# A planned attention and gated-MLP kernel: staging buffers, load shape and planner constants

## The chip, the cores and the metric

The kernel runs on one core of a Trainium2 chip. The metric is the device time of one launch in microseconds, as the median of several runs. One execution was also recorded by the hardware profiler; all durations below come from it.

## The reference, cut to what matters

Windowed attention with sink positions, and then a gated layer on its result. q, k and v are float32; the three weight matrices are 64-bit floats.

```python
# q, k, v: (4, 8, 768, 64); n_sink = 4, window = 128
scores = q @ k.T / sqrt(64)
keep   = (column < n_sink) | (0 <= row - column < window)
a      = softmax(where(keep, scores, -1e9))
x      = (a @ v)                       # reshaped to (3072, 512)
gate   = 1 / (1 + exp(-(x @ w_gate)))  # w_gate, w_val: (512, 1536)
out    = (gate * (x @ w_val)) @ w_out  # w_out: (1536, 512)
```

## The kernel before, in words

**Units of work.** A *head* here is one attention head over 256 rows of a batch: 4 batches x 3 row blocks x 8 heads = 96 of them (`attend`, numbered `u`). The first 20 (`PLAIN`) work in plain float32, which TensorE passes over four times; the others split each operand into a high part and a low part in the fast format (`copy` makes the high part, `rest` the low part) and add the products. The gated layer runs in 8 *chunks* of rows (`CHUNKS`, `feed`), each in 12 *slices* of 128 hidden columns. Chunk 0 (`feed_whole`) uses the unsplit weights `ws`; chunks 1 to 3 (`feed_plain`) use high and low parts; chunks 4 to 7 (`feed_pair`) take two row blocks together and save one product in eight.

**Weights.** Each slice has three blocks of raw 64-bit weights (gate, value, out; 512 KB each). `decode` loads a block into a staging buffer `wst` (three of them, `B_wst`), ScalarE scales its upper words (`ws<-wst`) and shifts 16-bit pieces (`wst<-wst`; VectorE or GpSimd may do that instead), and VectorE puts the bits together in `ws`. Later `halves` and `thirds` split the blocks; the low parts go out to a DRAM scratch `wlo_d` and are fetched back into eight buffers `lo` (`fetch`) for every slice of chunks 1 to 7.

**Order.** Nothing in the code says directly what stands behind what. Each operation is given to `Plan.op` with a priority, the engines that can do it with a duration for each, and the tiles it reads and writes. `Plan.run` then plays through all engines with these durations, takes on each free engine the ready operation of best priority, and writes the resulting order down; the chip executes each engine's list in that order. Constants fix how long a result needs to reach the next engine (`LAT`, the same for all), how a transfer's landing is reckoned (`BULK`, `ISSUE`), how long an input must have been there before TensorE takes its operation ahead of others (`SURE`, `SURE_D` behind a transfer), and when an engine of second choice may take an operation (`BACKA`, `BACKV`, `HOLD`, `GAP`). Up to `WARM` (130 us) the planner puts a *fill* into TensorE's list, a product of the identity with itself (`m<-ident`, two passes), wherever TensorE would stand idle while its activity is under `FLOOR`. Stores of `wlo_d`, loads of q and k (`qkT`), of v (`vraw`, `vhl`) and of weights all go through the one queue of SyncE (SP).

**End.** A flag tells whether the general path behind the last branch is needed; it is not here. `hint` places a branch hint for TensorE, VectorE and SyncE. In the last slice (`last_slice`) the four results `xf` are stored one by one.

Names as the trace shows them: `P` probabilities, `rs` their row sums, `wt` transposed probabilities, `th` and `cv` the gated layer's intermediate values, `gh` and `gl` their high and low part, `m`, `a`, `o` PSUM tiles, `xf` attention results and, at the end, the output rows.

Of the kernel before, what the change touches and what calls it, by code (L numbers as in the profile page):

```python
# [45 lines left out]
SINKP = -2.0  # L46
SCALP = -0.5
SKSWAP = 0
WHOLE = 1
DN1 = 36  # L50
DS1 = 8.0
DR1 = 0.2
DS2 = 18.0
DR2 = 0.3
KS1 = 16.0
KR = 0.9
KS2 = 25.0
XP = -900.0
ALT = 1
LAT = 180.0  # L60
BULK = 620.0
ISSUE = 550.0
SURE = 600.0
SURE_D = 1200.0
FREE = 150.0
NEXT = dict(PE=0.0, V=60.0, A=60.0, G=60.0, Q=0.0)
# [21 lines left out]
B_lo = 8  # L88
B_w2 = 2
B_wst = 3  # L90
# [222 lines left out]
class Plan:  # L313
# [39 lines left out]
    def run(self, warm, fill_ns, fill):  # L353
# [37 lines left out]
        while events:  # L391
            now = events[0][0]
            while events and events[0][0] <= now:
# [14 lines left out]
                for x in o.after:  # L408
                    x.before -= 1
                    same = len(x.ways) == 1 and x.ways[0][0] == on  # L410
                    x.ready = max(x.ready, now + (NEXT[on] if same else LAT))
                    if on != "PE":
                        x.sure = max(x.sure, now + LAT + (SURE_D if o.dma else SURE))
                    if not x.before:
                        n += 1
                        heapq.heappush(events, (x.ready, n, ("ready", x, None)))
            for e in free:
                if free[e] > now:
                    continue
                held = []  # L420
                unsure = [] if e == "PE" else None
                while waiting[e] or unsure:
# [18 lines left out]
                    if unsure is not None and (  # L441
                        o.sure > now
                        or any(slots[k][v - 1][1] + LAT + SURE > now for k, v in need.items())
                    ):
                        unsure.append((key, o))
                        continue
# [48 lines left out]
                    if through:  # L495
                        ns += max(0.0, port - now - LEAD)
                        port = now + ns + (70.0 if e == "V" else 0.0)
# [14 lines left out]
                    if o.dma:  # L512
                        slow = BULK if o.dma > 1000.0 else 0.0
                        dma_free = max(dma_free + o.dma, end + 650 + slow + o.dma)
                        end = dma_free + 750
# [8 lines left out]
                    for x in o.after:  # L524
                        x.todo -= 1
                        x.due = max(x.due, end + LAT)
# [23 lines left out]
def kernel(  # L550
# [13 lines left out]
    w_gate, w_val, w_out = (  # L564
        w.bitcast(I32).rearrange("r (c w) -> r c w", w=2) for w in (w_gate, w_val, w_out)
    )
    B, H, S, D = v.shape
    DM, DF, _ = w_gate.shape
    DO = w_out.shape[1]
    NC = DM // 128  # L570
    NF = DF // 128
# [267 lines left out]
    WLO, LOADS, GROUPS, DECODED, READY, READY2 = (Fixed(None) for _ in range(6))  # L839

    def sinks(b, u):
        if not b:
# [7 lines left out]
            for t, x in enumerate(VS0):  # L850
                for y in range(2):
                    o = 64 * y + NS * t
                    dma(
                        u + 0.5, 91.0, lambda x=x, y=y, o=o: Q.dma_start(
# [8 lines left out]
        for o in range(0, 128, NS):  # L863
            dma(
                u, 91.0, lambda o=o: Q.dma_start(
                    out=raw()[o : o + NS], in_=v[b, :, 0:NS, :].rearrange("h p d -> p h d"),
                ), [READY2], [(raw, o)] + [VSHL[b, i] for i in range(2) if b and (b, i) in VSHL],
# [10 lines left out]
    def load(u, b, h, t0, T, prev, L, vraw, vin, qkT, plain):  # L878
# [4 lines left out]
            u, 0.75 * n * R / D, lambda: Q.dma_start(out=qkT()[0:R, 0:n], in_=qk[b, h, 0:R, c0 : c0 + n]),  # L883
# [3 lines left out]
            u, 100.0 * L, lambda: Q.dma_start(  # L887
# [4 lines left out]
    def attend(u, b, h, t0, T, XR):  # L892
# [44 lines left out]
        for t in range(T):  # L937
# [28 lines left out]
            def exp(t=t):  # L966
# [5 lines left out]
            plan.op(u, [("PE", 10 + (4 * n / 2.4 + 6 if plain else 2 * mac(n)), scores)], qk_reads, [sc, (P, t)], busy=0.5 if plain else 0.9)  # L972
            plan.op(
                u, [("V", 260 if first else 535, top)],
                [sc, (MASKS, 3), (MASKS, min(t0 + t, 2))], [sc, (P, t), (NEGM, (u, t))],
            )
            plan.op(u, [("A", 410, exp)], [], [(P, t), (rs, t)])
# [19 lines left out]
        def mul():  # L997
            for t in range(T):
# [4 lines left out]
                ("A", 200, lambda: A.activation(  # L1003
                    out=rs()[:, 0:T], in_=rs()[:, 0:T], func=AF.Copy, scale=1.0, bias=1.0e-9
                )),
                ("G", Port(213), guard(G)), ("V", Port(100), guard(V)),
# [3 lines left out]
            u, [("V", 110, lambda: V.reciprocal(out=rs()[:, 0:T], in_=rs()[:, 0:T]))], [], [rs]  # L1010
        )
        plan.op(u, [("G", Port(660), share), ("A", 720, mul), ("V", Port(555), scale)], [rs], [P])

        if not plain:
# [11 lines left out]
                u, [("V", 180, lambda: V.transpose(  # L1026
# [10 lines left out]
                u, [("G", Port(610), spread(G)), ("V", two(W), spread(V))], [turned, OWN], [sk]  # L1037
# [35 lines left out]
        plan.op(u, [("PE", 30 + (T + plain) * 110, turn)], [P], [tp, wt], busy=0.45)  # L1073
# [11 lines left out]
        plan.op(u, [("G", Port(180 + 0.9 * Z * (T - f) * 128), split)], [], [wt])  # L1085
        plan.op(u, [("G", Port(180 + 0.9 * Z * T * 128), rest_of)], [], [wt])
# [105 lines left out]
        if y:  # L1192
# [8 lines left out]
            elif not pair_of[tn]:  # L1201
# [9 lines left out]
                copy(u, W, hi, xv, read, [(H1, i), (L1, i)], plain)  # L1211
# [44 lines left out]
    def decode(prio, src, whole):  # L1256
# [6 lines left out]
        plan.op(prio, [("Q", ISSUE, lambda: Q.dma_start(out=st(), in_=src))], [], [st], dma=1456.0)  # L1263
# [16 lines left out]
                ("G", Port(1340.0), lambda: G.tensor_scalar(  # L1280
# [26 lines left out]
    def weights(f, prio):  # L1307
# [11 lines left out]
    def spare(pr, f, k, x):  # L1319
        dma(  # L1320
            pr, 728.0, lambda: Q.dma_start(
# [5 lines left out]
    def halve(pr, f, k, shape, whole, r=(), start=0.0):  # L1327
        hi, lo = slot(F32R, shape), slot(F32R, shape)
        copy(pr, 512, hi, whole, [whole, *r], [hi, (lo, 0)], start=start)
# [43 lines left out]
    def out_tiles(ci, g, T, O):  # L1373

        for j, acc in enumerate(O):
# [15 lines left out]
            dma(ci, 728.0, lambda ot=ot, r=r: Q.dma_start(out=out[r : r + 128], in_=ot()), [ot])  # L1391
# [70 lines left out]
    def fetch(pr, f, *parts):  # L1462
        got = []
        for k in parts:
            x = tile([128, 512], F32R, "lo", BUFS["lo"], p3)
            LAST[0] = dma(
                pr, 728.0, lambda x=x, k=k: Q.dma_start(
# [93 lines left out]
    def feed_pair(ci, tcs, f, O):  # L1561
# [76 lines left out]
        gh, gl = gated(pr, 512, th)  # L1638
        downs(pe, f, O, gh, gl, woh, wol, (1.3, 1.5, 1.65, 1.7))

    def last_slice(pr, pe, O, th, cv, woh, wol):
# [23 lines left out]
        hint([(gh, 1)], [(th, 1)], [wol])  # L1665
# [153 lines left out]
```

## Time and profile before

| | |
|---|---|
| median of 3 runs | 775.3 us (772.66 to 777.56) |
| the profiled execution, its own time | 774.19 us |
| its span, first to last instruction | 772.5 us |
| TensorE busy with matmuls | 749.1 us, 97% |
| VectorE, ScalarE, GpSimd busy | 607.5, 472.0, 506.1 us |
| granted TensorE clock | 0.998 |
| moved by DMA | 185.57 MB, mean 240 GB/s |

TensorE is "busy" whenever a matmul is in its pipe, so its share says that it is seldom empty. An engine's idle time counts only where TensorE, or the last store, waits for it.

### The profile page before, as it was taken

What the parts mean: (1) busy time and instruction counts of PE and PEld (TensorE: products, weight loads), DVE (VectorE), ACT (ScalarE), POOL (GpSimd) and SP (SyncE); (2) the same over time, 40 slices, a digit from 0 to 9 for tenths busy, and PEclk for the clock granted to TensorE, in tenths of its full rate; (3) what the DMA queues carried; (4) which work ended last, traced back from release to release, by engine and by line L of the source; (5) the groups of instructions that cost most, each with busy time, mean ns of one, the idle gap of its engine ahead of it and who ended that gap; (6) DMA issues with size and microseconds to landing.
All of it is one profiled execution on the core that took longest, in us unless ns stands there. A gap on an engine that the chain in (4) does not pass through costs nothing.

```text
span 772.5 us, 16296 instructions
## 1 busy us (share of the span) xinstructions
PE 749.1 (97%) x4986; PEld 674.9 (87%) x4986; DVE 607.5 (79%) x1782; ACT 472.0 (61%) x1338; POOL 506.1 (66%) x647
## 2 busy tenths in 40 slices
PE   7999999999999999999999999999999999999995
PEld 6866777998989999989999988999999999999995
DVE  5979988996999999969988889778999884433333
ACT  7879888765765777737666665457776652322221
POOL 3654676887999999937777977557976855321210
PEclk9999999999999999999999999999999999999999
DMA  6898987999999877677767777867697655677662
GB/s 165 222 297 250 323 263 234 376 307 311 342 294 319 284 220 207 200 252 231 233 224 225 242 233 222 246 196 251 193 306 249 196 159 178 217 240 211 198 205 86
DMA packets 120879, 185.57 MB, mean 240 GB/s; under 512 B 23248, under 2 KB 45264, under 8 KB 120784
## 3 DMA queue, kind: packets, MB, share of 16 engines
q1 hardware_dynamic: 120784, 184.45, 75.9%
q8 instruction: 42, 0.69, 0.4%
q14 instruction: 53, 0.43, 0.2%
HBM read 159.24 MB, written 25.17 MB: 239 GB/s over the span
## 4 chain that ended last, share of the span: by engine, by line
PE 61%; DVE 11%; DMA 6%; POOL 3%; ACT 2%; issue 2%; SPq 0%; ACTq 0%; POOLq 0%; DVEq 0%
PE m L620 34%; PE a L620 16%; PE o L620 11%; DVE ws L620 2%; DMA wst<-in_moe_w_gate_dram 1%; DMA out_dram<-w 1%; DVE P L620 1%; DVE th L620 1%; DMA vraw<-in_vt_dram 1%; DMA lo<-wlo_d 1%; DVE vhl L620 1%; POOL wt L620 1%; DVE hi L620 1%; DVE gl L620 1%; DVE xf L620 1%
## 5 line engine op out<-in xcount | busy, mean ns | idle before, releaser
L620 PE MATMUL m<-ws,ws 128*128 128x256 f32 x1536 | 290.0, 284 | 0.6 <-DVE th L620 0.2
L620 PE MATMUL m<-ws,lo 128*128 128x256 f32 x1344 | 288.6, 283 | 1.9 <-DMA lo<-wlo_d 1.3
L620 PEld LDWEIGHTS m<-ws,ws 128*128 128x128 f32 x1536 | 244.9, 189 | 13.1 <-DVE th L620 1.0
L620 PEld LDWEIGHTS m<-ws,lo 128*128 128x128 f32 x1344 | 215.0, 189 | 3.1 <-DMA lo<-wlo_d 2.3
L620 POOL TENSOR_SCALAR_AFFINE_SELECT wt<-wt 128x512 fp32r<-128x512 f32 (+3 forms) x192 | 125.9, 657 | 43.5 <-DVE wt L620 18.7
L620 POOL TENSOR_TENSOR gl<-th,gh 128x512 fp32r<-128x512 f32 (+1 forms) x34 | 38.2, 1122 | 99.6 <-ACT gh L620 82.7
L620 ACT ACTIVATE P<-P,negm_all 128x144 f32<-128x144 f32 x192 | 78.9, 412 | 28.7 <-DVE negm_all L620 26.8
L620 ACT ACTIVATE th<-m 128x256 f32<-128x256 f32 x96 | 36.6, 382 | 75.5 <-DVE th L620 71.9
L620 DVE TENSOR_TENSOR cv<-m,cv 128x256 f32<-128x256 f32 x96 | 40.2, 418 | 52.4 <-ACT cv L620 34.8
L620 ACT CAST gh<-th 128x512 fp32r<-128x512 f32 (+1 forms) x82 | 42.9, 523 | 55.3 <-DVE th L620 53.7
L620 POOL TENSOR_TENSOR ws<-ws,ws 128x512 fp32r<-128x512 f32 (+1 forms) x53 | 66.6, 1262 | 9.8 <-DVE ws L620 6.9
L620 PE MATMUL o<-ws,gh 128*128 128x512 f32 x168 | 67.6, 403 | 0.0
L620 PE MATMUL o<-ws,gl 128*128 128x512 f32 x168 | 66.2, 394 | 0.0
L620 PE MATMUL o<-lo,gh 128*128 128x512 f32 x168 | 65.8, 391 | 0.0
L620 DVE CUSTOM_DVE_ANT_0 P<-a,am 128x144 f32<-128x144 f32 x192 | 58.3, 306 | 8.8 <-PE a L620 2.2
L620 PE MATMUL a<-wt,vhl 128*128 128x256 f32 (+2 forms) x282 | 61.0, 327 | 1.8 <-POOL wt L620 1.6
L620 POOL TENSOR_TENSOR kl<-qkT,hi 128x400 fp32r<-128x400 f32 (+1 forms) x56 | 59.2, 1057 | 1.8
L620 PEld LDWEIGHTS a<-wt,vhl 128*128 128x128 f32 x282 | 47.3, 189 | 10.5 <-POOL wt L620 4.1
L620 ACT CAST hi<-qkT 128x656 fp32r<-128x656 f32 (+1 forms) x70 | 49.2, 703 | 10.9 <-PE a L620 10.0
L620 POOL TENSOR_TENSOR P<-P,rs 128x288 f32<-128x288 f32 x46 | 35.1, 764 | 29.8 <-DVE rs L620 26.2
L620 POOL TENSOR_TENSOR hi<-qkT,hi 64x256 fp32r<-64x256 f32 x53 | 41.2, 777 | 14.9 <-issue 4.9
L620 DVE COPY_PREDICATED a<-tri,a 128x128 f32<-128x128 int32 x160 | 45.4, 284 | 3.5 <-PE a L620 3.2
(146 smaller groups left out, 1735.5 us busy)
## 6 DMA issues: line engine op xcount, KB each, us to landing
lo<-wlo_d SPq DMA_DIRECT2D x396, 256.0 KB, 3.7
wlo_d<-ws SPq DMA_DIRECT2D x72, 256.0 KB, 4.3
qkT<-in_qk_dram SPq DMA_DIRECT2D x52, 328.0 KB, 4.1
qkT<-in_qk_dram SPq DMA_DIRECT2D x24, 264.0 KB, 3.5
wst<-in_moe_w_gate_dram SPq DMA_DIRECT2D x12, 512.0 KB, 4.8
wst<-in_moe_w_val_dram SPq DMA_DIRECT2D x12, 512.0 KB, 5.1
wst<-in_moe_w_out_dram SPq DMA_DIRECT2D x12, 512.0 KB, 5.4
out_dram<-w SPq DMA_DIRECT2D x20, 256.0 KB, 4.4
```

The source lines that it names most:

```text
L620: return lambda *a, **kw: tc.keep_in_program_order(op(*a, **kw))
```

## The change

Five things. (1) `w_gate` and `w_val` are laid out by the host as (slice, partition, 4, 128), so that a load reads one run of 4 KB per partition where it read four of 1 KB; `w_out` had runs of 4 KB before. (2) Four staging buffers instead of three. (3) The planner: one latency `LAT` becomes a sum by engines (`AFTER`, `TOLD`) with a margin (`SLACK`, behind a transfer `DSLACK`); landing times are reckoned from `REACH` and `LANDED`; SyncE's list gets no further transfer while the planned line of transfers is longer than `REACH + QUEUED`; durations of ScalarE, GpSimd, VectorE and TensorE operations are set anew; GpSimd takes an operation of VectorE only if it would wait there for `BACKV` = 300 ns (0 before). (4) `GUARD`, `SPLIT`: from chunk 3 on, the high and low parts of x wait in the plan for the splitting of all weights; splitting starts later (`HALVED`, `THIRDS`). (5) The branch hint stands five slices earlier in the last chunk.

```diff
-BACKV = 0.0
+BACKV = 300
-HOLD = 0.6
+HOLD = 0.8
-GAP = 2.0
+GAP = 4.0
-HALVED = 30000.0
+HALVED = 40000.0
-THIRDS = 130000.0
+THIRDS = 140000.0
-DS1 = 8.0
-DR1 = 0.2
+DS1 = 7
+DR1 = 0.25
-LAT = 180.0
-BULK = 620.0
-ISSUE = 550.0
-SURE = 600.0
-SURE_D = 1200.0
+AFTER = dict(PE=163.0, V=75.0, A=100.0, G=35.0, Q=0.0)
+TOLD = dict(PE=54.0, V=35.0, A=35.0, G=77.0, Q=27.0)
+REACH = 2000.0
+LANDED = 430.0
+SLACK = 100
+DSLACK = 300
+QUEUED = 1000
+ISSUE = 480.0
+SURE = 900
+SURE_D = 1200
-B_wst = 3
+B_wst = 4
...
-                    x.ready = max(x.ready, now + (NEXT[on] if same else LAT))
+                    lat = AFTER[on] + TOLD[x.ways[0][0]] + (DSLACK if o.dma else SLACK)
+                    x.ready = max(x.ready, now + (NEXT[on] if same else lat))
...
+                if e == "Q" and dma_free > now + REACH + QUEUED:
+                    n += 1
+                    heapq.heappush(events, (dma_free - REACH - QUEUED, n, None))
                     continue
...
-                        dma_free = max(dma_free + o.dma, end + 650 + slow + o.dma)
-                        end = dma_free + 750
+                        dma_free = max(dma_free, now + REACH) + o.dma
+                        end = dma_free + LANDED
...
     def act(cols, psum=False):
-        return 120 + 0.9 * cols
+        return 28 + 0.93 * cols
 
     def pool(cols):
-        return Port(170 + 2.17 * cols)
+        return Port(135 + 2.17 * cols)
...
-                copy(u, W, hi, xv, read, [(H1, i), (L1, i)], plain)
+                copy(u, W, hi, xv, read + [SPLIT] * (ci > WHOLE + GUARD), [(H1, i), (L1, i)], plain)
...
-            decode(prio(), w[:, fs].rearrange("(c p) f w -> p c f w", p=128), whole)
+            decode(prio(), w[f], whole)
...
         gh, gl = gated(pr, 512, th)
+        if ci == len(CHUNKS) - 1 and f == NF - 6:
+            hint([gh], [th], [wol])
...
-        hint([(gh, 1)], [(th, 1)], [wol])
...
+    for name in ("moe_w_gate", "moe_w_val"):
+        made[name] = inputs[name].reshape(4, 128, -1, 128).transpose(2, 1, 0, 3)
```

What the planner makes of it is seen in the order of the instructions. SyncE's list near its start, before (`wst` a staging buffer, `qkT` q and k of a head, `vhl` v of a head, `w` raw sink values):

```order
L620 DMA qkT_121<-in_qk_dram 64x528
L620 DMA wst_197<-in_moe_w_gate_dram 128x4x256
L620 DMA wst_202<-in_moe_w_val_dram 128x4x256
L620 DMA wst_209<-in_moe_w_out_dram 128x1024
L620 DMA w_215<-in_v_dram 16x8x64 x3
L620 DMA qkT_165<-in_qk_dram 64x528
L620 DMA w_215<-in_v_dram 16x8x64
L620 DMA vhl_116<-in_vt_dram 128x2x64
L620 DMA qkT_103<-in_qk_dram 64x528
```

The same place after the change:

```order
L630 DMA wst_183<-in_moe_w_gate_dram 128x1024
L630 DMA qkT_121<-in_qk_dram 64x528
L630 DMA wst_200<-in_moe_w_val_dram 128x1024
L630 DMA wst_211<-in_moe_w_out_dram 128x1024
L630 DMA qkT_154<-in_qk_dram 64x528
L630 DMA wst_242<-in_moe_w_gate_dram 128x1024
L630 DMA vhl_116<-in_vt_dram 128x2x64
L630 DMA qkT_103<-in_qk_dram 64x528
L630 DMA vhl_149<-in_vt_dram 128x2x64
L630 DMA w_282<-in_v_dram 16x8x64
L630 DMA wst_292<-in_moe_w_val_dram 128x1024
```

The second slice's gate block stood 14 rows behind the first slice's; now it stands five rows behind, and the raw sink values have moved back behind it.

TensorE's list at the eighth head, before (`m<-ident` is a fill, `a<-ident,P` a transpose of probabilities, `a<-qkT` scores, `a<-wt,vhl` and `a<-sk,vshl` probabilities times v):

```order
L620 MATMUL a_459<-ident,P_393 128x128 x2
L620 MATMUL a_459<-ident,P_393 32x128
L620 MATMUL m_91<-ident 128x128
L620 MATMUL a_470<-qkT_103 128x272
L620 MATMUL a_473<-qkT_103 128x272
L620 MATMUL a_484<-wt_435,vhl_144 128x256
L620 MATMUL a_484<-wt_435,vhl_144 128x128
L620 MATMUL m_91<-ident 128x128
L620 MATMUL a_484<-wt_467,kl_160 128x256
L620 MATMUL a_484<-wt_467,kl_160 128x128
```

After:

```order
L630 MATMUL m_91<-ident 128x128 x4
L630 MATMUL a_488<-ident,P_417 128x128 x2
L630 MATMUL a_488<-ident,P_417 32x128
L630 MATMUL m_91<-ident 128x128
L630 MATMUL a_500<-wt_464,vhl_134 128x256
L630 MATMUL a_500<-wt_464,vhl_134 128x128
L630 MATMUL a_508<-qkT_103 128x272
L630 MATMUL a_511<-qkT_103 128x272
L630 MATMUL m_91<-ident 128x128 x5
L630 MATMUL a_500<-wt_503,kl_152 128x256
L630 MATMUL a_500<-wt_503,kl_152 128x128
```

The same products are there, with ten fills where there were two.

The last rows of SyncE's list before the final branch, before (`lo` a low part, `xf` output rows):

```order
L620 DMA lo_11244<-wlo_d 128x512
L620 DMA lo_11249<-wlo_d 128x512
L620 DMA lo_11263<-wlo_d 128x512
L1814 BRANCH_PREFETCH_HINT
L620 DMA out_dram<-xf_11357 128x512
L620 DMA out_dram<-xf_11360 128x512
L620 DMA out_dram<-xf_11364 128x512
L620 DMA out_dram<-xf_11368 128x512
```

After:

```order
L630 DMA lo_11266<-wlo_d 128x512
L630 DMA lo_11274<-wlo_d 128x512
L630 DMA lo_11282<-wlo_d 128x512
L630 DMA out_dram<-xf_11373 128x512
L630 DMA out_dram<-xf_11375 128x512
L630 DMA out_dram<-xf_11381 128x512
L630 DMA out_dram<-xf_11385 128x512
```

The hint now stands 26 rows ahead of the first of these stores.

## Rows read from the trace of the kernel before

**Rows 1.** The page, part 1: busy time, share of the span, instructions of each engine.

```profile
PE 749.1 (97%) x4986; PEld 674.9 (87%) x4986; DVE 607.5 (79%) x1782; ACT 472.0 (61%) x1338; POOL 506.1 (66%) x647
```

**Rows 2.** Windows: start:end, length, busy us of PE, PEld, DVE, ACT, POOL; clock; DMA.

```profile
0.00:34.50 34.50, 29.07 (x179) 25.89 (x180) 24.29 (x108) 27.58 (x84) 16.97 (x39) 1.00 0.73 186
34.50:131.80 97.30, 92.63 (x423) 68.38 (x422) 85.11 (x229) 85.43 (x167) 56.98 (x68) 1.00 0.89 273
131.80:191.90 60.10, 58.84 (x414) 54.02 (x413) 50.48 (x127) 37.50 (x114) 50.93 (x62) 1.00 0.97 329
191.90:255.60 63.70, 63.33 (x443) 57.78 (x442) 58.47 (x156) 42.05 (x127) 59.78 (x73) 1.00 0.95 316
255.60:323.70 68.10, 67.83 (x488) 63.15 (x487) 64.98 (x224) 52.77 (x177) 63.12 (x84) 1.00 0.75 230
323.70:437.40 113.70, 112.00 (x789) 104.14 (x788) 97.08 (x289) 69.20 (x210) 81.52 (x107) 1.00 0.73 231
437.40:554.70 117.30, 115.80 (x812) 107.45 (x811) 100.22 (x311) 72.08 (x225) 84.92 (x113) 1.00 0.73 227
554.70:667.10 112.40, 112.25 (x788) 104.23 (x787) 89.43 (x265) 61.78 (x187) 76.38 (x96) 1.00 0.68 215
667.10:760.20 93.10, 93.09 (x647) 86.67 (x645) 33.80 (x72) 21.80 (x51) 15.53 (x12) 1.00 0.65 203
760.20:772.50 12.30, 4.31 (x20) 3.19 (x18) 3.66 (x8) 1.80 (x5) 0.00 (x0) 0.87 0.25 91
```

**Rows 3.** Timeline of TensorE, 0 to 36 us: start, length, what; in brackets idle before.

```profile
6.53 1.05 PE L620 MATMUL m<-ident 128*128 128x128 f32 x8
9.49 0.55 PE L620 MATMUL a<-ident,P 128*128 128x128 f32 x3 [1.91 <-POOL P L620]
...
18.34 0.94 PE L620 MATMUL a<-qkT 128*128 128x144 f32 x4 [1.63 <-DMA qkT<-in_qk_dram]
...
34.52 1.67 PE L620 MATMUL m<-xf,ws 128*128 128x256 f32 x7
```

**Rows 4.** Waits of TensorE's matmuls, whole span: releaser, us in total, times, longest.

```profile
PE a L620 <- POOL P L620: 3.3, 4, 1.9
PE a L620 <- POOL wt L620: 1.8, 4, 0.6
...
PE m L620 <- DMA lo<-wlo_d: 1.3, 2, 1.0
```

**Rows 5.** Waits of TensorE's weight loads, whole span.

```profile
PEld a L620 <- POOL P L620: 6.5, 10, 2.1
...
PEld a L620 <- POOL wt L620: 4.8, 11, 0.9
...
PEld m L620 <- DMA lo<-wlo_d: 2.3, 4, 1.2
```

**Rows 6.** Groups by shape, TensorE and ScalarE: count, busy us, mean ns, idle before.

```profile
L620 PE MATMUL m<-ident 128*128 128x128 f32 x52 | 9.9, 317 | 1.4 <-POOL ident masks.py:199 1.4
...
L620 ACT ACTIVATE wst<-wst 128x512 uint16<-128x512 uint16 x34 | 46.2, 1360 | 0.5
...
L620 ACT ACTIVATE ws<-wst 128x512 f32<-128x512 f32 x35 | 24.0, 685 | 9.4 <-DMA wst<-in_moe_w_val_dram 5.4 <-DMA wst<-in_moe_w_gate_dram 2.1 <-DMA wst<-in_moe_w_out_dram 1.7
```

**Rows 7.** The tile `th`: ns of one, min/median/max, first and last start.

```profile
L620 DVE TENSOR_TENSOR gl<-th,gh x51: 382/707/1114, 138.7 to 762.2; 128x256 fp32r<-128x256 f32 x26, 128x512 fp32r<-128x512 f32 x25
...
L620 POOL TENSOR_TENSOR gl<-th,gh x34: 729/1293/1307, 141.1 to 754.6; 128x512 fp32r<-128x512 f32 x22, 128x256 fp32r<-128x256 f32 x12
```

**Rows 8.** DMA issues: count, KB each, median us to landing.

```profile
wst<-in_moe_w_gate_dram SPq DMA_DIRECT2D x12, 512.0 KB, 4.8
...
wst<-in_moe_w_out_dram SPq DMA_DIRECT2D x12, 512.0 KB, 5.4
```

**Rows 9.** The last stores, by their tile: ns of one issue, min/median/max.

```profile
L620 SPq DMA_DIRECT2D out_dram<-xf x4: 338/654/1547, 764.1 to 766.9; - x4
```

**Rows 10.** Timeline of VectorE, its last instruction.

```profile
764.96 0.42 DVE L620 TENSOR_SCALAR xf<-o 128x256 f32<-128x256 f32 x1 [0.28 <-ACT xf L620]
```

More of the change, by code (lines that the diff above doesn't have):

```diff
@@ L88 @@
 B_lo = 8
+GUARD = 1
 B_w2 = 2
-B_wst = 3
+B_wst = 4
 B_a = 4
@@ L442, in run @@
                         o.sure > now
-                        or any(slots[k][v - 1][1] + LAT + SURE > now for k, v in need.items())
+                        or any(slots[k][v - 1][1] + AFTER["V"] + TOLD["PE"] + SURE > now for k, v in need.items())
                     ):
@@ L496, in run @@
                         ns += max(0.0, port - now - LEAD)
-                        port = now + ns + (70.0 if e == "V" else 0.0)
+                        port = now + ns + AFTER[e]
                     if e == "PE":
@@ L635, in act, with moved @@
     def act(cols, psum=False):
-        return 120 + 0.9 * cols
+        return 28 + 0.93 * cols
     def pool(cols):
-        return Port(170 + 2.17 * cols)
+        return Port(135 + 2.17 * cols)
+    def moved(n, size):
+        return n * (16 + size / 24.0)
     def mac(cols):
@@ L838 @@
     X0 = {}
-    WLO, LOADS, GROUPS, DECODED, READY, READY2 = (Fixed(None) for _ in range(6))
+    WLO, SPLIT, GROUPS, DECODED, READY, READY2 = (Fixed(None) for _ in range(6))
     def sinks(b, u):
@@ L864, in sinks @@
             dma(
-                u, 91.0, lambda o=o: Q.dma_start(
+                u, moved(8, 256), lambda o=o: Q.dma_start(
                     out=raw()[o : o + NS], in_=v[b, :, 0:NS, :].rearrange("h p d -> p h d"),
-                ), [READY2], [(raw, o)] + [VSHL[b, i] for i in range(2) if b and (b, i) in VSHL],
+                ), [READY2], [(raw, o)] + [(VSHL[b, i], o) for i in range(2) if b and (b, i) in VSHL],
             )
@@ L882, in load @@
         dma(
-            u, 0.75 * n * R / D, lambda: Q.dma_start(out=qkT()[0:R, 0:n], in_=qk[b, h, 0:R, c0 : c0 + n]),
+            u, (1040.0 if plain else 890.0) * n / 656, lambda: Q.dma_start(out=qkT()[0:R, 0:n], in_=qk[b, h, 0:R, c0 : c0 + n]),
             w=[(qkT, 0)], start=0.0 if plain else LATER,
@@ L886, in load @@
         dma(
-            u, 100.0 * L, lambda: Q.dma_start(
+            u, moved(8 * L, 256) if plain else moved(8, 256 * L), lambda: Q.dma_start(
                 out=vin(), in_=vt[b, h, :, k0 // 128 : k0 // 128 + L]
@@ L1036, in attend @@
             plan.op(
-                u, [("G", Port(610), spread(G)), ("V", two(W), spread(V))], [turned, OWN], [sk]
+                u, [("G", Port(568), spread(G)), ("V", two(W), spread(V))], [turned, OWN], [sk]
             )
@@ L1071, in rest_of @@
             )
-        plan.op(u, [("PE", 30 + (T + plain) * 110, turn)], [P], [tp, wt], busy=0.45)
+        plan.op(u, [("PE", 20 + T * 60 + 190 * plain, turn)], [P], [tp, wt], busy=0.45)
         plan.op(
@@ L1328, in halve @@
         hi, lo = slot(F32R, shape), slot(F32R, shape)
-        copy(pr, 512, hi, whole, [whole, *r], [hi, (lo, 0)], start=start)
+        copy(
+            pr, 512, hi, whole, [whole, *r], [hi, (lo, 0)] + [(SPLIT, (f, k))] * (k > 2), start=start
+        )
         rest(pr, 512, lo, whole, hi, [whole, hi], [(lo, 0)])
@@ L1390, in out_tiles @@
                 plan.op(-1000.0 + ci + 1, ways if last else ways[:1], [acc], [ot])
-            dma(ci, 728.0, lambda ot=ot, r=r: Q.dma_start(out=out[r : r + 128], in_=ot()), [ot])
+            dma(ci, moved(8, 2048), lambda ot=ot, r=r: Q.dma_start(out=out[r : r + 128], in_=ot()), [ot])
     def feed(ci):
```

56 lines of the change are left out of this document (28 added, 28 removed).

## The prediction

> **What bounds the kernel now.** I read the parts of the page first. TensorE is busy for 749.1 us of 772.5, 97% [rows 1]; no other engine is over 79%. The change neither removes nor adds a product of the reference: counted in the two printed orders, every form of matmul stands as often as before, except the fills. So the time after is the same TensorE work, plus the fills, plus whatever TensorE waits, plus the end behind its last matmul. What can be won is the waiting, and the windows by stage say how much that is [rows 2]. I cut them where the second half of the first slice's gate product begins (34.5), where chunk 0 ends (131.8), and then about at each chunk's last slice. Length less busy time gives TensorE's idle time: 5.43 us up to 34.5; 4.67 in the rest of chunk 0; 1.26, 0.37, 0.27, 1.70, 1.50, 0.15 and 0.01 in the seven later stages; 7.99 in the end. Sum 23.35. The granted clock is 1.00 in every stage but the end, so no clock can be won.
>
> The timeline of the start [rows 3] shows a chain: 1.91 us for the first probabilities, 1.63 us for a load of q and k. The lists of waits show what the rest is made of: matmuls waited 3.3 us for `P`, 1.8 for `wt`, 1.3 for low parts from DRAM [rows 4]; the weight loads ahead of them waited 6.5, 4.8 and 2.3 us for the same three [rows 5]. Those larger sums are partly covered by the matmul still running, so they bound the visible 23.35 us from above, and are not added to it.
>
> **The change part by part.** All terms are us against the profiled execution's own 774.19 (span 772.5 and 1.7 around it). The median of the runs shown is 1.1 above it, well within their scatter of 5.
>
> *Rows of 4 KB.* 24 of the 36 weight loads become like the other 12. Those already read 4 KB runs and land in 5.4 us, the 1 KB ones in 4.8 [rows 8]. So shorter landing is not to be expected: 0, and at the best the 0.6 us the other way is noise. TensorE does not wait on these loads by name at all; ScalarE does, for 9.4 us in all [rows 6].
>
> *Four staging buffers, earlier weights.* The second slice's gate block comes five rows behind the first, not 14. By the printed orders ScalarE does 9 instead of 5 decoding steps before its 16th exponential, and 40 instead of 28 before the 32nd. Four steps at a mean of 0.685 and 1.360 us [rows 6] are about 4.1 us of ScalarE, in a stage where it is busy for 27.58 of 34.50 [rows 2]: the first heads come up to 4.1 us later. The planner puts fills there: 43 instead of 26, all within the first nine heads. A run of four took 1.05 us, so 0.26 each [rows 3], and 17 are 4.5; 26 fills were busy 9.9 [rows 6], 0.38 each, 6.5 for 17. Where they stand in a wait they cost nothing. Bounds 0 and +6.5; I take +2, nearer to the lower end, since the heads of that stage are waited for anyway. In return the slices of chunk 0 find their weights ready, and the 4.67 us of idle time behind 34.5 can go. Bounds 0 and -4.7; I take -3.
>
> *Planner durations and margins.* The new constants say that a result takes 75 + 35 + 100 = 210 ns from VectorE to ScalarE and 163 + 35 + 100 = 298 ns from TensorE to VectorE, before 180 for all; behind a transfer 300 are added, and TensorE's margin grows from 600 to 900. A wider margin makes TensorE take something else first, and there is something else: products of the gated layer. The waits that this touches are the visible 5.25 us from 131.8 to 667.1 and what lies hidden in the weight loads' waits [rows 2, 5]. Bounds: 0, and the visible 5.25 plus the weight loads' excess over the matmuls for the three releasers, (6.5 - 3.3) + (4.8 - 1.8) + (2.3 - 1.3) = 7.2, in all 12.4. I take -5, a little under the visible part: the longest single waits go, and short ones stay.
>
> *Work moved from GpSimd to VectorE* (`BACKV`). Of the 85 subtractions `gl`, VectorE has 76 instead of 51; GpSimd's list shrinks from 647 to 564 rows, ScalarE's grows from 1142 to 1178. On the path: 0 as long as VectorE has room, and it has 3 to 23 us in each stage of the later chunks [rows 2]. Its cover goes if a stage asks more of VectorE than TensorE takes; that is the rival below. The rows show that VectorE's subtraction has no fixed length: 382 to 1114 ns over two shapes [rows 7]. The Trainium skill, "SBUF — State Buffer", section "Who interferes with whom", says that VectorE with two SBUF inputs and a GpSimd operation that reads SBUF exclude each other for a whole instruction. The spread in the row fits that. By this rule fewer GpSimd instructions also make VectorE's quicker, and the sum would stay 767; with VectorE's lengths as they are, the extra work counts in full and the rival's 781 comes nearer.
>
> *The hint, and the last stores.* SyncE issued four stores in 338 ns at the quickest, 654 in the middle and 1547 at the slowest [rows 9], at the point where VectorE's last instruction ended at 765.38 [rows 10] while the last store was only issued at 766.9. Behind that the end is the landing. Without the slow issue the last store goes out about 1.2 us sooner (1547 - 338). Whether the hint just ahead of the stores makes it slow, no row says: bounds 0 and -1.2; I take -1.
>
> *The short line of transfers, `GUARD`, later splitting.* They move SyncE's list. TensorE waits on low parts for 1.3 us in all [rows 4], counted above. 0.
>
> Sum: 774.2 + 2 - 3 - 5 - 1 = 767.2, so **767**.
>
> **The rivals.**
>
> *The start gives it back.* The 17 fills cost their full 4.5 because they delay the head behind them, the 4.1 us of earlier decoding are on the chain, so nothing of the 4.67 is won: 774.2 + 4.5 - 5 - 1 = 772.7, about **773**. For it: ScalarE is the fullest helper of that stage. Against it: TensorE has the slices of chunk 0 to go on with as soon as weights are there.
>
> *VectorE becomes the bound* (slower). In the printed order the second chunk's stage holds 12 heads instead of 6. Compare the stage 437.4 to 554.7 (12 slices and 17 heads) with 667.1 to 760.2 (12 slices, none): a head costs VectorE (100.22 - 33.80) / 17 = 3.9 us and TensorE (115.80 - 93.09) / 17 = 1.3 [rows 2]. Six more heads in the stage from 131.8 make VectorE 50.48 + 23.4 = 73.9 and TensorE 58.84 + 8.0 = 66.8: 7 us that TensorE waits and that a later, emptier stage does not return. With the fills at 4.5 and the planner's gain of 5 gone: 774.2 + 4.5 - 3 + 7 - 1 = 781.7, about **782**. It decides if a plain-chunk head costs VectorE more than (66.8 - 50.5) / 6 = 2.7 us; heads of the pair chunks, from which 3.9 is taken, carry additions that these lack, and GpSimd has less to do.
>
> *Everything that can go, goes.* Fills stand in waits (0), the 4.67 are gone, the planner's part is 9, the stores 1.2: 774.2 - 4.7 - 9 - 1.2 = **759**. For it: the waits are for many small hand-overs, which one cause can remove. Against it: `P` and `wt` are waited for at the start too, where no other work is ready.
>
> **How the numbers follow.** The forecast (767, own range 763 to 772) has 0.50, the start that gives it back 0.22, VectorE as the bound 0.13, the large gain 0.15. A difference of 1% is about what a measurement of this kernel can tell from none: against the median, under 767.5 or over 783.1, and I count the case of 782 as slower by over 1% since its price may well be higher. Faster: all of the large gain and a little over half of the forecast, 0.15 + 0.28 = 0.43. Slower: 0.13. Same: the rest, 0.44. For 8 in 10 the range takes in the forecast, the start's case with its unknown (773 and 4 more) and the large gain with 1 below: 758 to 777.
>
> **What would show it.** Fills: 86 instead of 52 records of `m<-ident`, and the first `m<-xf,ws` later than 34.52; if it comes earlier, decoding was not on the chain. Chunk 0 ends at about the same time as before (131.8), with less idle time behind the start. TensorE's visible waits for `P`, `wt` and `lo` behind 131.8 under 2 us. VectorE busy for under 97% of the second chunk's stage; if it is full there and TensorE's waits name VectorE, the rival has come true. The last four stores without an issue over 1 us, and an end (behind TensorE's last matmul) of about 7 instead of 8 us. I am wrong if TensorE's busy time, less fills, has moved by more than 3 us, since then the pace of matmuls themselves has changed, which no term here holds.

## The result, and the profile after

The changed kernel takes **763.4 us** (median of 4 runs, 762.29 to 763.88). The kernel before took 774.98 (4 runs beside it, 772.66 to 777.56). The ratio is 0.9848, with a 95% interval of 0.9814 to 0.9881: 1.5% faster. The forecast was 767, with a range of 758 to 777. Its own time in the profiled execution is 763.68, against 774.19 before.

Part 1 of the page of the kernel after: busy time and share of the span (762.0 us), and instructions of each engine.

```profile
PE 746.6 (98%) x5020; PEld 679.3 (89%) x5020; DVE 618.4 (81%) x1796; ACT 479.4 (63%) x1378; POOL 454.8 (60%) x592
```

Against [rows 1], GpSimd has lost 51 us of work, VectorE has gained 11, ScalarE 7. TensorE is busy 2.5 us less although it has 34 more records of fills.

Windows of the kernel after, cut at the same points of the program as [rows 2]: the first slice's second half of the gate product, the end of chunk 0, then the twelfth slice of each chunk. Columns: start:end, length, busy us of PE, PEld, DVE, ACT, POOL; granted clock; DMA share; GB/s.

```profile
0.00:38.60 38.60, 32.90 (x210) 29.52 (x211) 29.82 (x113) 33.28 (x89) 22.37 (x41) 1.00 0.87 223
38.60:132.50 93.90, 93.24 (x446) 71.66 (x444) 85.44 (x225) 87.38 (x199) 60.52 (x71) 1.00 0.94 301
132.50:196.00 63.50, 63.50 (x457) 59.21 (x456) 58.26 (x186) 49.40 (x161) 56.56 (x81) 1.00 0.85 272
196.00:251.30 55.30, 54.81 (x389) 50.90 (x389) 46.65 (x108) 33.54 (x96) 44.66 (x49) 1.00 0.96 323
251.30:317.50 66.20, 66.10 (x479) 62.15 (x477) 58.14 (x197) 45.85 (x153) 48.33 (x65) 1.00 0.78 244
317.50:433.10 115.60, 114.52 (x807) 106.66 (x808) 103.75 (x313) 75.45 (x235) 83.18 (x109) 1.00 0.73 234
433.10:547.60 114.50, 114.44 (x808) 106.80 (x807) 102.25 (x313) 70.34 (x218) 79.50 (x105) 1.00 0.74 235
547.60:657.30 109.70, 109.70 (x774) 102.68 (x773) 87.46 (x250) 60.57 (x179) 59.69 (x76) 1.00 0.68 212
657.30:750.70 93.40, 93.40 (x651) 87.11 (x650) 43.35 (x92) 21.90 (x51) 0.00 (x0) 1.00 0.64 204
750.70:762.00 11.30, 3.94 (x16) 2.57 (x15) 3.25 (x7) 1.73 (x4) 0.00 (x0) 0.90 0.27 99
```

Three things are to be seen. The second half of the first slice's gate product begins 4.1 us later (38.6 against 34.5), but the rest of chunk 0 is 3.4 us shorter, with 0.66 us of idle TensorE instead of 4.67: chunk 0 ends at 132.5, practically where it ended before (131.8). From there to the end it took 640.7 us and now takes 629.5. So the whole gain of the span, 10.5 us, lies behind chunk 0. In the stage after chunk 0 VectorE is busy for 58.26 of 63.50 us, 92%, and TensorE never stands.

Waits of TensorE's matmuls from 133 us to the end, kernel after: releaser, us in total, times, longest.

```profile
PE m L630 <- DMA lo<-wlo_d: 0.6, 2, 0.3
PE a L630 <- DVE negm_all L630: 0.5, 1, 0.5
PE o L630 <- DVE gl L630: 0.3, 1, 0.3
PE a L630 <- DVE sk L630: 0.2, 1, 0.2
```

That is the whole list: 1.6 us in 5 waits. The same list of before sums to 4.4 us in 11. Its three largest:

```profile
PE m L620 <- DMA lo<-wlo_d: 1.3, 2, 1.0
PE a L620 <- POOL P L620: 0.8, 2, 0.5
PE a L620 <- POOL wt L620: 0.6, 1, 0.6
```

`P` and `wt` are not waited for any more here. Most of what [rows 4] gives for these two, over the whole span, lay ahead of 133 us.

**Why idle time shows only part of it.** The idle time of TensorE's windows fell by 7.9 us (23.35 to 15.45), the span by 10.5. Eight records of fills in a row take 1.05 us [rows 3], and one takes 0.30, so one begins every 0.11 us and its neighbours overlap it. A gap of up to some 0.2 us between two starts is thus counted as busy. I therefore worked out from all matmul records how far each start lies from the next one's, and took off the usual distance for that shape (of all such distances in the trace of before, in order of size, the one a third of the way up). What is left is called *lost time* below. How large it comes out hangs on the distance that is called usual, so it is the differences between kernels that are read. Before it is 51.4 us, after 37.6.

| us | start | rest of chunk 0 | behind chunk 0 |
|---|---|---|---|
| lost time before | 8.7 | 11.2 | 31.5 |
| lost time after | 9.8 | 5.0 | 22.8 |

The books close: 13.8 less lost, 0.7 less behind the last matmul (8.0 to 7.3), and 34 more records of fills at 0.11, 3.7, make 10.8; the span says 10.5. Of the 11.2 us behind chunk 0, lost time is 8.7, the end 0.7, and about 1.3 is one head that now stands in chunk 0 (TensorE has the scores of 24 heads behind it at its end instead of 23).

### The profile page after: what moved, and what is told of

Read it like the earlier page. It is cut to its first block, busy times and chain, and to the rows that moved or that the text cites. A ratio compares the mean times of both kernels' runs of the same rounds, so it can differ in the third digit from the quotient of the medians.

```text
span 762.0 us, 16324 instructions
## 1 busy us (share of the span) xinstructions
PE 746.6 (98%) x5020; PEld 679.3 (89%) x5020; DVE 618.4 (81%) x1796; ACT 479.4 (63%) x1378; POOL 454.8 (60%) x592
## 2 busy tenths in 40 slices
DMA packets 111661, 185.55 MB, mean 244 GB/s; under 512 B 23248, under 2 KB 32976, under 8 KB 111568
## 4 chain that ended last, share of the span: by engine, by line
PE 78%; DVE 7%; ACT 7%; DMA 5%; issue 2%; SPq 1%; POOL 1%; DVEq 0%; ACTq 0%
PE m L630 43%; PE a L630 20%; PE o L630 15%; DVE ws L630 2%; ACT wst L630 2%; ACT ws L630 2%; ACT P L630 1%; DMA wst<-in_moe_w_gate_dram 1%; DMA lo<-wlo_d 1%; DMA wst<-in_moe_w_val_dram 1%; SPq L630 1%; DMA wst<-in_moe_w_out_dram 1%; DVE P L630 1%; DVE xf L630 1%; DMA qkT<-in_qk_dram 0%
## 5 line engine op out<-in xcount | busy, mean ns | idle before, releaser
L630 PEld LDWEIGHTS m<-ws,ws 128*128 128x128 f32 x1536 | 242.4, 189 | 8.8 <-issue 0.5
L630 POOL TENSOR_SCALAR_AFFINE_SELECT wt<-wt 128x512 fp32r<-128x512 f32 (+3 forms) x192 | 128.1, 668 | 56.9 <-DVE wt L630 38.2
L630 POOL TENSOR_TENSOR kl<-qkT,hi 128x400 fp32r<-128x400 f32 (+1 forms) x60 | 63.1, 1053 | 13.9 <-ACT hi L630 11.8
L630 DVE TENSOR_TENSOR gl<-th,gh 128x512 fp32r<-128x512 f32 (+1 forms) x76 | 52.3, 689 | 13.1 <-ACT gh L630 10.7
L630 POOL TENSOR_TENSOR hi<-qkT,hi 64x256 fp32r<-64x256 f32 x57 | 45.2, 794 | 19.0 <-issue 6.4
L630 ACT CAST hi<-qkT 128x656 fp32r<-128x656 f32 (+1 forms) x67 | 47.2, 704 | 12.1 <-PE a L630 10.2
```

The lines of the kernel that those rows point to most:

```text
L630: return lambda *a, **kw: tc.keep_in_program_order(op(*a, **kw))
```

## The experiments

Two theories. **Planner:** the gain comes from one or more of the planner's constants, which put less work in front of results that aren't there; undoing that part gives its share back. **Other parts:** loads, buffers, fills or the hint carry it. A third had to be kept apart from both, **luck of the order:** any small change of a constant deals all five lists anew, and the time scatters from one deal to the next.

### Rows of 1 KB again

The host's layout and the access pattern are those of before; the order of all lists is the same.

```diff
-            decode(prio(), w[f], whole)
+            decode(prio(), w[:, fs].rearrange("(c p) f w -> p c f w", p=128), whole)
...
```

> The changed kernel with one part undone: the gate and value weights are again read in four runs of 1 KB per partition. Every engine's list keeps its order, so the load shape stands alone. Mine (4 KB rows are worth nothing, the unsplit runs landed no later): 763 to 764 us, and the landing of the 24 loads within 0.5 us of the changed kernel's 5.3 to 5.5. Rival (the transfers crowd the early stage, and shorter ones free it): 766 or more, and the first product of the second half of slice one later than 38.6.

Measured: 764.24 us (763.5 to 764.5), 0.9876 of before (0.986 to 0.9893). DMA issues of this kernel (KB each, median us to landing), and then of the kernel after:

```profile
wst<-in_moe_w_gate_dram SPq DMA_DIRECT2D x12, 512.0 KB, 5.4
wst<-in_moe_w_val_dram SPq DMA_DIRECT2D x12, 512.0 KB, 5.5
```

```profile
wst<-in_moe_w_gate_dram SPq DMA_DIRECT2D x12, 512.0 KB, 5.5
wst<-in_moe_w_val_dram SPq DMA_DIRECT2D x12, 512.0 KB, 5.3
```

The 9,216 packets fewer (111,661 after, 120,877 here) buy nothing. The second half of the first slice's gate product begins at 40.0 us here and not at 38.6, as the rival expected, but the time that went with it (766 or more) did not come, and the next run has such a later start (39.6) with TensorE's list unchanged up to that point. The shape of the rows is worth 0.

### The hint at its old place

```diff
-        if ci == len(CHUNKS) - 1 and f == NF - 6:
-            hint([gh], [th], [wol])
...
+        hint([(gh, 1)], [(th, 1)], [wol])
```

> The changed kernel with the branch hint back in the last slice, just ahead of the stores; TensorE's list differs in four rows, GpSimd's in none. Mine: the end behind TensorE's last matmul is 1 us longer (8.0 instead of 7.3), total 764 to 765. Rival (the slow issue of a store comes from elsewhere, it is still there with the early hint, 1330 ns): end and total unchanged, 763 to 764.

Measured: 763.75 us (762.41 to 764.48), 0.987 (0.9851 to 0.9889). The last stores, ns of one issue as min/median/max, first of this kernel, then of the kernel after:

```profile
L630 SPq DMA_DIRECT2D out_dram<-xf x4: 338/396/1419, 753.8 to 756.2; - x4
```

```profile
L630 SPq DMA_DIRECT2D out_dram<-xf x4: 338/395/1330, 753.9 to 756.2; - x4
```

One slow issue stands there with the hint just ahead of it and with the hint 26 rows away. The hint is not its cause, and its place is worth nothing.

### The 16 extra fills left out

Of the 43 fills (86 records) the last 16 are not written down. This leaves out products whose result nobody reads; all else keeps its place.

```diff
+        seen = 0
...
-            fn()
+            seen += o is None
+            if o is not None or seen <= 26:
+                fn()
```

> The changed kernel with its last 16 fills left out of the list (27 of 43 stand); every other instruction keeps its place, and the reference's work is all done. If the fills stand in waits, as most of my term of +2 said: the first product of the second half of slice one stays at 38.6 and the time at 763 to 764.5. If they push the heads behind them (the rival's 0.26 us each): about 4 us earlier, 34.5 to 36, and 759 to 761. If they hold the clock: the granted clock falls under 1.00 between 25 and 45 us and the time rises over 766.

Measured: 763.67 us (762.9 to 765.36), 0.9871 (0.9835 to 0.9908): the same as with them. The end of chunk 0 doesn't move either (132.6 against 132.5). So the extra fills stood in waits. What else they did is seen in the windows of 24 to 32 us, first without them, then with them (the clock is the third figure from the end of a row):

```profile
24.00:28.00 4.00, 2.40 (x15) 1.83 (x13) 1.82 (x8) 3.18 (x9) 2.33 (x3) 1.00 1.00 246
28.00:32.00 4.00, 3.90 (x16) 3.54 (x17) 3.08 (x9) 3.85 (x11) 2.38 (x5) 0.57 1.00 258
```

```profile
24.00:28.00 4.00, 3.33 (x23) 2.87 (x22) 3.84 (x13) 3.95 (x14) 3.48 (x6) 1.00 1.03 271
28.00:32.00 4.00, 4.00 (x30) 3.65 (x30) 3.78 (x10) 3.81 (x10) 3.50 (x5) 1.00 1.03 232
```

Without them TensorE is busy for 2.40 us of 4, and in the next 4 us the clock is granted at 0.57, near the lower of its two levels, 1.2 GHz. The second half of the first slice's gate product then begins at 40.0 instead of 38.6, and not at 38.6 as was expected if fills stand in waits. But 1.0 of these 1.4 us says nothing on fills: in the run with the hint at its old place, which has them all and a clock of 1.00 in these windows, it begins at 39.6. And chunk 0 takes the delay up again: the time did not rise over 766, as was expected if the fills hold the clock.

### One hand-over time of 180 ns for all, and 182 ns

Both give the planner one time for every hand-over again, with the old `SURE` and `NEXT`; they differ by 2 ns in the constant, to see two deals of the same thing.

```diff
-SURE = 900
+SURE = 600
-NEXT = dict(PE=0.0, V=10.0, A=25.0, G=0.0, Q=0.0)
+NEXT = dict(PE=0.0, V=60.0, A=60.0, G=60.0, Q=0.0)
...
-                    lat = AFTER[on] + TOLD[x.ways[0][0]] + (DSLACK if o.dma else SLACK)
+                    lat = 180.0
...
```

> The changed kernel with the planner's hand-over times put back: one latency of 180 ns for all, no margins by engine, SURE 600, the old NEXT; durations, buffers and row shape stay new. Theory 1 (the gain behind 40 us comes from truthful hand-overs and wider margins): 768 to 772, and TensorE's lost time behind 130 us goes back to near that of before. Theory 2 (it comes from earlier weights and four buffers): 763 to 765. Theory 3 (any new order of this planner scatters, and this one fell well): anywhere within 759 to 770, not told by this run alone.

> A second sample of the kernel with the old hand-over times (182 ns for all, SURE 600), so that the scatter of orders does not decide. If the hand-over times bring the gain behind chunk 0, the time from the end of chunk 0 to the end is again near the 641 to 646 us of the kernels with the old planner (the first sample had 640.4), total 769 to 775, while TensorE's lost time inside chunk 0 stays near 4 to 5 us. If the first sample was only an unlucky order: 627 to 637 from chunk 0 to the end, total 761 to 767.

Measured: 770.88 us (766.37 to 773.32), 0.995 (0.9927 to 0.9973) with 180, and 768.54 (766.58 to 769.55), 0.9939 (0.9918 to 0.9959) with 182. Chunk 0 ends earlier than after (130.2 and 128.6), the stretch behind it takes longer (640.4 and 636.3 us, against 629.5). The second run lies between what its two theories expected (641 to 646 us behind chunk 0, or 627 to 637, and 769 to 775 or 761 to 767 in all). Whether that is the hand-over times or the deal, the next runs say.

### Neutral deals

One constant moved by a hair, for no purpose but a new order: in the changed kernel `LANDED` 430 to 435, `SURE` 900 to 905 and to 880; in the kernel before `BULK` 620 to 625, `ISSUE` 550 to 555.

```diff
-SURE = 900
+SURE = 905
```

> The changed kernel with one constant moved by next to nothing: LANDED 435 instead of 430 ns. It means nothing for the chip, but the planner's order comes out anew (some 1200 of 4920 rows of TensorE stand elsewhere). It measures how far the time scatters by order alone. Theories 1 and 2: within 2 us of the changed kernel, 761 to 766. Theory 3 (luck of the order): off by 4 us or more, one way or the other.

> A second new order of the changed kernel from a constant that means nothing to the chip: SURE 905 instead of 900 ns. After LANDED 435 gave 771.0, theory 3 (the planner's orders scatter by several us, and the changed kernel is a lucky one) expects 765 to 773 again, on average of the neighbours about 769. The other theory (the changed planner's orders are good, 435 was an unlucky exception) expects 761 to 766.

> A third such order: SURE 880 instead of 900 ns. As for SURE 905: theory 3 expects 765 to 773, the other 761 to 766.

> The kernel before with one of its own constants moved by next to nothing: BULK 625 instead of 620 ns; TensorE's list differs in some 1200 rows. If the whole gain is luck of the order, neighbours of the kernel before scatter around the same middle as those of the changed one: 764 to 774. If the change has a systematic part beside the luck, they stay at 770 to 780.

> A second neighbour of the kernel before: ISSUE 555 instead of 550 ns. All luck: 764 to 774. A systematic part: 770 to 780.

Measured, with the lost time behind chunk 0 and the length of that stretch from each one's profiled execution:

| kernel | median us | ratio to before (95%) | behind chunk 0 | lost there |
|---|---|---|---|---|
| after | 763.4 | 0.9848 (0.9814 to 0.9881) | 629.5 | 22.8 |
| after, `SURE` 905 | 761.71 | 0.986 (0.9824 to 0.9896) | 627.2 | 20.4 |
| after, `SURE` 880 | 764.67 | 0.9892 (0.9861 to 0.9924) | 631.3 | 24.1 |
| after, `LANDED` 435 | 771.01 | 0.9973 (0.995 to 0.9996) | 636.8 | 29.9 |
| before | 774.98 | 1 | 640.7 | 31.5 |
| before, `ISSUE` 555 | 777.39 | 1.0067 (1.004 to 1.0094) | 643.0 | 34.1 |
| before, `BULK` 625 | 779.85 | 1.0092 (1.0064 to 1.0121) | 645.6 | 37.2 |

The deal alone is worth 9.3 us between the best and the worst of the changed kernel's four, and 4.9 among the three of before (6.3 against the 773.54 that the kernel before took beside its two neighbours). The means are 765.2 and 777.4, 12.2 apart, and no median of the one family reaches into the other. So the gain as a whole is the change's, not luck, though 1.8 us of it, the distance of this deal from the mean of its family, may be; and a single deal doesn't measure a part of it to better than some 4 us. `SURE` 905 is the quickest kernel here, though its ratio lies within the interval of the kernel after. The times of 770.88 and 768.54 for the old hand-over times lie inside the four neutral deals (761.7 to 771.0). Behind chunk 0 the first of the two, with 640.4 us, lies above all four (627.2 to 636.8), the second, with 636.3, among them. Their share isn't shown.

### Three staging buffers

```diff
-B_wst = 4
+B_wst = 3
```

> The changed kernel with three staging buffers. If the fourth buffer brings the smaller waiting inside chunk 0 (4 to 6 us against 11 with the old planner): 9 to 12 us lost there and chunk 0 ends at 136 or later. If the planner's durations and hand-overs bring it: 4 to 7 us lost, end at 131 to 134. Behind chunk 0 nothing should change but by the scatter of orders: 627 to 637 us. Total by the first 766 to 772, by the second 761 to 771.

Measured: 773.19 us (769.0 to 774.12), 0.9976 (0.9953 to 0.9999). Where chunk 0 ends, by the last start of its last product (`o<-ws,th`; ns of one as min/median/max, first and last start), first in the kernel after, then here:

```profile
L630 PE MATMUL o<-ws,th x48: 592/592/697, 43.0 to 132.5; 128*128 128x512 f32 x48
```

```profile
L630 PE MATMUL o<-ws,th x48: 590/592/697, 47.8 to 137.5; 128*128 128x512 f32 x48
```

As a whole this can't be told from the slowest neutral deal (0.9973). Half of the 10 us is lost up to the end of chunk 0 (5.0), half behind it (634.3 against 629.5 us), and the second half is within what a deal does there (up to 636.8). The first is not: in the four deals with four buffers chunk 0 ends between 132.0 and 134.1. In this one deal three buffers thus cost 3 to 5 us up to there. The two stretches, cut at 42.8 us, where the second half of the first slice's gate product begins here:

```profile
0.00:42.80 42.80, 35.11 (x212) 31.18 (x213) 29.40 (x119) 33.49 (x88) 19.69 (x40) 0.96 0.73 199
42.80:137.50 94.70, 93.18 (x452) 72.84 (x451) 83.12 (x227) 90.28 (x194) 73.66 (x84) 1.00 0.88 278
```

4.2 of the 5.0 us are lost before that point (42.8 against 38.6). In the rest of chunk 0 TensorE stands idle for 1.52 us, against 0.66 after and 4.67 before. So the run bears out neither theory whole: chunk 0 ends at 136 or later, as the theory of the fourth buffer said, but most of the smaller waiting inside it is there without that buffer. And part of the later start may be the clock's, which from 28 to 32 us was granted at 0.64 here; no run parts the two.

### The old durations

Operations of ScalarE, GpSimd and VectorE and two of TensorE get the lengths that the planner of before had, and so does the time that it adds behind an operation until the port that it reckons with (`port`) is free; all else is as after.

```diff
-        return 28 + 0.93 * cols
+        return 120 + 0.9 * cols
...
-        return Port(135 + 2.17 * cols)
+        return Port(170 + 2.17 * cols)
...
-                        port = now + ns + AFTER[e]
+                        port = now + ns + (70.0 if e == "V" else 0.0)
...
```

> The changed kernel with the old durations of the engines (ScalarE 120 + 0.9 a column, GpSimd 170 + 2.17 and so on), the new hand-over times kept. If truthful durations matter as much as hand-overs: 638 to 646 us from chunk 0 to the end, total 768 to 776. If the hand-over times alone do it: 627 to 637, total 760 to 768.

Measured: 774.08 us (773.09 to 777.16), 1.0009 (0.9989 to 1.0029): the whole gain is gone, and more than the slowest neutral deal gave up, if by little: 774.1 against 771.0, with intervals of the ratio that still overlap, and it is one deal. Part 1 of its page, and the longest of its matmul waits from 133 us on:

```profile
PE 751.6 (97%) x5030; PEld 683.0 (88%) x5030; DVE 636.1 (82%) x1846; ACT 472.7 (61%) x1342; POOL 455.2 (59%) x580
```

```profile
PE a L630 <- DVE negm_all L630: 1.9, 3, 1.1
PE m L630 <- DVE th L630: 1.1, 2, 0.9
PE o L630 <- DVE gl L630: 0.9, 1, 0.9
PE m L630 <- DVE cv L630: 0.8, 2, 0.6
PE m L630 <- DVE ws L630: 0.8, 1, 0.8
```

Chunk 0 ends at 133.0, as after; the stretch behind it takes 641.1 us (11.6 more), with 34.1 us lost. ScalarE has 36 instructions fewer than after, VectorE 50 more. Of 7.5 us of visible waits behind chunk 0, 6.2 name VectorE; in the kernel after it is 1.0 of 1.6, and in the slowest neutral deal 2.1 of 6.8. A planner that believes ScalarE slow hands its work to VectorE, and in this deal TensorE waits there. In the kernel before, which had the same durations, GpSimd took such work (647 instructions in [rows 1], 580 here), with `BACKV` at 0. The counts and the waits show where the work went and who was waited for; that this explains all of the 11.6 us is argued, since a deal alone can be worth 7 (629.5 to 636.8).

With three buffers and with the old durations 9.8 and 10.7 us of a gain of 11.6 are given back. Whether the parts need each other or the deals were poor ones is open. The stops `GUARD` and `SPLIT`, `BACKV` alone and the short line of transfers were not tried by themselves, nor were constants that stand where the listing of the change is cut: the priorities `SINKP` and `KR` and the durations of transfers (`moved`).

## Why the prediction came out right, step by step

- **TensorE bounds it, and only waiting can be won.** Right. The most frequent form has the same length before and after:

```profile
L620 PE MATMUL m<-ws,lo 128*128 128x256 f32 x1344 | 288.6, 283 | 1.9 <-DMA lo<-wlo_d 1.3 <-issue 0.4
```

```profile
L630 PE MATMUL m<-ws,lo 128*128 128x256 f32 x1344 | 289.6, 282 | 0.6 <-DMA lo<-wlo_d 0.6
```

- **"I am wrong if TensorE's busy time, less fills, has moved by more than 3 us".** It has moved by 7.1 (749.1 - 9.9 = 739.2 to 746.6 - 14.5 = 732.1), and yet the two most frequent forms have kept theirs within 1 ns, and no form's mean moved by more than 13 ns. The sign was badly chosen: the part of the page counts overlapped matmuls once, so small gaps that vanish make busy time fall. Summed form by form, busy time rose by 4.1 us, of which the fills are 4.6 (14.5 - 9.9): all other forms together moved by half a microsecond.
- **4 KB rows, 0.** Right, and borne out by the run with 1 KB rows.
- **Four buffers, earlier weights: +2 for fills, -3 for chunk 0's idle time.** The net of -1 was right: chunk 0 ends 0.6 later, with one head (1.3) more in it. The inside was not. The fills are free (the run without them), not +2; there are 86 records as forecast:

```profile
L630 PE MATMUL m<-ident 128*128 128x128 f32 x86 | 14.5, 304 | 1.4 <-POOL ident masks.py:199 1.4
```

  The first `m<-xf,ws` at 38.6 is 4.1 us later, the very figure of the forecast, though other executions and neighbours of the changed kernel have it at up to 40.0; it counts in full, while it stood there only as an "up to". The idle time of the rest fell by 4.0 of 4.67, and that pays for it. ScalarE's decoding up to that point, in the kernel before and then after (count, busy us, mean ns):

```profile
L620 ACT ACTIVATE wst<-wst 128x512 uint16<-128x512 uint16 x3 | 4.1, 1358 | 0.0
L620 ACT ACTIVATE ws<-wst 128x512 f32<-128x512 f32 x5 | 3.4, 689 | 0.4 <-DMA wst<-in_moe_w_gate_dram 0.2 <-DMA wst<-in_moe_w_val_dram 0.2
```

```profile
L630 ACT ACTIVATE wst<-wst 128x512 uint16<-128x512 uint16 x7 | 9.5, 1358 | 0.0
L630 ACT ACTIVATE ws<-wst 128x512 f32<-128x512 f32 x9 | 6.0, 669 | 2.5 <-DMA wst<-in_moe_w_gate_dram 1.3 <-DMA wst<-in_moe_w_val_dram 1.1
```

  These are 16 steps, 15.5 us, where before there were 8, 7.5 us. But the cause named for it, the fourth buffer, is wrong: with three buffers there are 15 steps before that point, which comes later still, at 42.8. The seven kernels with all of the new planner and four buffers have 16 and reach it at 38.6 to 40.0; the three of the old planner have 8 and reach it at 34.5 to 36.6. So the planner's constants bring the weights forward. Neither the hand-over times nor the durations do it alone: with the one or the other undone there are still 15 and 17 steps. That the eight more steps make the start late is argued, not shown: with 15 it came at 37.7, 39.6 and 42.8.
- **Planner durations and margins, -5.** That TensorE waits less, and the place (behind chunk 0, on many small hand-overs), were right, the size was not: about -9 there (lost time 31.5 to 22.8). That the wider margins do it, by letting TensorE take something else first, is not shown. The bounds of 0 and -12.4 held it only because the excess of the weight loads' waits, 7.2, was taken from lists of the whole span, start and all, for a term that begins at 131.8. From 132 to 668 us before, the weight loads waited:

```profile
PEld m L620 <- DMA lo<-wlo_d: 2.1, 3, 1.2
PEld a L620 <- POOL P L620: 1.9, 4, 0.7
PEld a L620 <- POOL wt L620: 1.0, 2, 0.8
```

  Against 1.3, 0.8 and 0.6 us of the matmuls there, that is an excess of 2.3, and a bound of 7.6, which lost time passed. (Nor can three sums that make 13.6 bound 23.35 us from above.) I stayed under the visible idle time of 5.25. Two thirds of that went (1.73 is left), and more again lay in gaps that overlapping matmuls hide. The Trainium skill, "Perfetto Trace Analysis", section "Identifying the Most-Contended Engine", says that matmul busy time is a poor measure of headroom, because matmuls are pipelined. Here the trace agrees: 13.25 us of idle time behind chunk 0 stood before, 4.2 of it went, and the stretch became 11.2 shorter. Visible waits for `P`, `wt` and `lo` are 0.6 us there (forecast: under 2; before 2.7). Which constant earns it stays open: undoing the durations costs the most, but in one deal; undoing the hand-over times can't be told from a neutral deal.
- **Work moved to VectorE, 0.** Right. The five more heads of the stage after chunk 0 came with 7.8 us more on VectorE (58.26 - 50.48), 1.6 each, where the rival took 3.9 and needed 2.7. It was mis-priced from the pair chunks. VectorE did become what TensorE waits for, with 6.2 us of waits, in the deal with the old durations. GpSimd's list went from 647 to 592 instructions; the 564 of the forecast is a count of the printed order, set against 647 from the trace. The subtraction `gl` on VectorE by shape, before and then after (count, busy us, mean ns):

```profile
L620 DVE TENSOR_TENSOR gl<-th,gh 128x512 fp32r<-128x512 f32 x25 | 20.6, 824 | 1.8 <-ACT gh L620 1.2 <-POOL kl L620 0.2 <-PE a L620 0.2
L620 DVE TENSOR_TENSOR gl<-th,gh 128x256 fp32r<-128x256 f32 x26 | 17.4, 670 | 2.4 <-ACT gh L620 1.4 <-PE o L620 1.0
```

```profile
L630 DVE TENSOR_TENSOR gl<-th,gh 128x512 fp32r<-128x512 f32 x40 | 30.9, 773 | 9.9 <-ACT gh L630 9.4 <-PE a L630 0.2
L630 DVE TENSOR_TENSOR gl<-th,gh 128x256 fp32r<-128x256 f32 x36 | 21.4, 597 | 3.1 <-ACT gh L630 1.3 <-PE o L630 0.8 <-ACT ws L630 0.7
```

  There are 76 of them as forecast, and in each shape they are quicker, by 51 and 73 ns. Laid beside GpSimd's records, the 40 of 128x512 after fall into two sets: the 15 with no GpSimd instruction beside them took 692 to 694 ns, the 25 others 662 to 1235, 821 in the mean. Before, all 25 had one beside them, and their mean was 824. By the rule cited from the Trainium skill, "SBUF — State Buffer", "Who interferes with whom", they should be quicker with less on GpSimd; the trace agrees.
- **Hint and last stores, -1.** Wrong in its reason. The issue of over 1 us is still there (1330 ns). The end got 0.7 shorter, about what the four issues together took less (3.19 us before, 2.46 after); why the third and fourth are quicker is open. With the old place of the hint the end is 7.4.
- **The rivals.** *The start gives it back* (773) named the later start rightly, and it is true of chunk 0 by itself; it was wrong that the fills cost. *Everything goes* (759) had the planner's 9 and the free fills right, and missed that the later start eats the 4.0 won in chunk 0: 759 and 4.1 make 763. What neither the forecast nor a rival held is the deal: the four lie from 3.5 us under their mean to 5.8 over it, which a range of 758 to 777 took in without naming it. With `LANDED` at 435 the same change would have gained 0.3%. That the forecast of 767 came within 4 us is thus in part luck: the later start cost 4.1 that no term held, and against it the fills cost 2 less, the rest of chunk 0 gave 1 more and the planner's part some 4 more. And another deal of the same constants took 771.0.

## What to carry to other kernels

Where a planner or scheduler deals the order, run two or three neighbours with a constant moved by a hair before a gain is put down to a part: here that scatter was 9 us, near the whole gain, and of the parts undone one by one none came out clear of it. Look where a planner sends the work when a length in it is wrong: with ScalarE priced too long, VectorE had 50 instructions more, and in that deal TensorE waited for it. Where matmuls overlap, idle time understates what waiting costs; measure start to start against the usual distance of that form.

## What the runs showed of the hardware

Of the four last stores one was issued slowly in all but one of the fourteen profiled kernels, for 1130 to 1804 ns where the quickest took 338, wherever the hint stood; its cause stays open. Weight loads of 512 KB landed in 4.8 and 5.1 us in the kernel before and in 5.3 to 5.5 in the changed one with either row length, so the run length does not set it. The output weights, whose rows had 4 KB all along, rose with them, from 5.4 to 5.9; what does set it isn't shown. VectorE's subtraction of two tiles of 128x512 took 692 to 694 ns in the 15 cases with no GpSimd instruction beside it, and up to 1235 ns in the 25 others (kernel after). And 16 products that nobody reads cost nothing in their waits, while without them TensorE's clock was granted at 0.57 for one stretch of 4 us.
